# Attention's PSUM banks as eight tiles instead of four pairs, two small steps on other engines, and the order made anew

## Chip, core and metric

The kernel runs on one core of a Trainium2 chip, as one program. The metric is the device time of one execution in microseconds; the kernel before took 1075.49 us (median of three runs).

## What is computed

Three layers follow each other, all in float32. Attention works on 8 batches of 8 heads, 576 positions, 64 columns a head and 128 random features; the two dense layers on a width of 512.

```
phi(x):  proj = x @ w_phi;  proj -= max|proj| over the features;  concat(exp(proj), exp(-proj))
kv  = phi(k)^T @ v          z = sum over positions of phi(k)
x   = (phi(q) @ kv) / (phi(q) . z + 1e-6)              heads put side by side: (8, 576, 512)

xk, xr = mu_k*x + (1-mu_k)*x_prev,  mu_r*x + (1-mu_r)*x_prev     x_prev: one position earlier
x   = sigmoid(xr @ w_r) * (relu(xk @ w_k)^2 @ w_v)

gate = sigmoid(causal convolution of x over 5 positions, per column)
out  = (gate * (x @ w_val)) @ w_out
```

The weights of the dense layers and of the convolution come as 64-bit floats, read as pairs of int32.

## The kernel before

**Attention** goes over 32 pairs of heads (`NP`), two of them to a loaded block of q, k and v. For each pair TensorE projects q and k with `w_phi` (L556), VectorE takes the largest absolute value of each row (`TENSOR_REDUCE`, L562) and subtracts it (L564), ScalarE takes the exponentials. The centred q is turned by TensorE first (L621) and its exponentials are taken out of PSUM (L625). Then come `kv` (L662), `num` (L696), their copies out of PSUM (L321), a division on GpSimd and VectorE (L713, L715, L718) and the turn back (L736).

**PSUM** is held as four tiles of `[128, 2, 512]`, each two banks of 512 floats. Attention takes single banks: half `place % 2` of tile `place // 2`. The class `Banks` hands them out. The dense layers take a whole tile, one half for each half of the positions.

**The weights** are brought from 64 bits to 32 while attention runs, in 28 pieces of `[128, 512]` that `fetch` loads. `narrow` makes five steps of each: an absolute value on ScalarE (L362, `s0`), a clamp to the range of exponents on GpSimd (L365, `s1`), and three steps on VectorE (L368, L372, L376, `s2` to `s4`). GpSimd then splits the piece into a rounded part and a rest (L413, L407) for the dense products.

**The dense layers** go over 8 batches (iterations `it`), each with 624 products of 128x128 by 128x288 (L831): `st_k`, `st_r`, `st_val` of the batch before, `st_v`, and `st_out` of the batch before. The moving operands of `st_k` and `st_v` are made just in time in the tile `ops`: a rounded copy by ScalarE (L815) and the rest by VectorE (L324). `prep` loads a batch's x into the tile `xb`, whose column 0 of each of four blocks is zero (the position before the first) and is set by a memset on VectorE (L912); the load fills columns 1 to 576 of each block.

**What sets the order.** The class `Order` collects every step with its engine, a cost in microseconds, a wished time and what it reads and writes; `run` then plays the steps forward by these costs and emits, engine by engine, the one that could start first. `SEM` and `SAME` are the costs of a hand-over to another engine and to the same; `SPLIT` is added where TensorE changes to another division of its array ("rows" for the projection, "columns" for `kv` and `num`). Every engine runs its queue in the order in which it was emitted. The waits between engines are not `Order`'s: they are put in afterwards, from the tiles that each instruction touches.

```python
banks = [psum.tile([128, 2, 512], F32, tag=f"b{i}", name=f"b{i}", bufs=1) for i in range(4)]
b.places, b.tile = [place], self.pairs[place // 2][:, place % 2]
```

Of the kernel before, what the change touches and what calls it, by code (L numbers as in the profile page):

```python
# [38 lines left out]
SEM = 0.2  # L39
SAME = 0.13  # L40
# [5 lines left out]
SPLIT = 0.29  # L46
KV = 0.125
SOON, EARLY = 0.6, 0.8

# [11 lines left out]
class Banks:  # L61


    def __init__(self, pairs, most):
        self.most, self.held, self.pairs = most, [], pairs

    def when(self, tasks, new):

        live, found, out = dict.fromkeys(self.most, 0), [], set(range(2 * len(self.pairs)))
        for b in self.held:  # L70
            out.difference_update(b.places)
            ends = [tasks[u]["end"] for u in b.users]
            if None in ends:
                live[b.tag] += 1
            else:
                found += [(max(ends) + SEM, k, b) for k in b.places]
# [4 lines left out]
        if any(b.tag in LAST for b in new) and sum(live[x] for x in LAST) >= 2 * len(self.pairs):  # L81
            return None
        found = sorted([(0.0, i, None) for i in out] + found, key=lambda f: f[:2])
        if new[0].wide:
# [5 lines left out]
            return [(t, k, at[k][2]), (t, k + 1, at[k + 1][2])]  # L90
        return found[:len(new)] if len(found) >= len(new) else None

    def take(self, found, new):
        for old in {id(f[2]): f[2] for f in found if f[2] is not None}.values():
            self.held.remove(old)
        if new[0].wide:
            b = new[0]
            b.places, b.tile = [f[1] for f in found], self.pairs[found[0][1] // 2]
            self.held.append(b)
            return  # L100
        for (_, place, _), b in zip(found, new):
            b.places, b.tile = [place], self.pairs[place // 2][:, place % 2]
            self.held.append(b)
# [12 lines left out]
class Order:  # L116
# [6 lines left out]
    def add(self, eng, dur, fn, r=(), w=(), new=(), at=None, dma=0, split=False):  # L123
# [12 lines left out]
        for b in new:  # L136
            self.queue.setdefault(b.tag, []).append((b, t["id"]))
        for x in itertools.chain(r, w):
            b = x[0] if isinstance(x, tuple) else x
            if isinstance(b, Buf):  # L140
                b.users.append(t["id"])
                t["bufs"].add(b)
        t["deps"].discard(t["id"])
        self.tasks.append(t)

    def run(self):
# [3 lines left out]
        free, dma_free = {}, 0.0  # L150
        todo = {}
# [5 lines left out]
        def ready(t):  # L157
            at = 0.0
            for d in t["deps"]:
                d = tasks[d]  # L160
                if d["end"] is None:
                    return None
                at = max(at, d["end"] + (SEM if d["eng"] != t["eng"] else 0.0 if t["eng"] == "PE" else SAME))
# [9 lines left out]
            for b in t["new"]:  # L173
# [7 lines left out]
                if old >= 0:  # L181
                    for u in self.queue[b.tag][old][0].users:
                        u = tasks[u]
                        if u["end"] is None:
                            return None
                        at = max(at, u["end"] + SEM)
            return at

        left, split = len(tasks), False
        while left:  # L190
            best = None
            for eng, q in todo.items():
                f = free.get(eng, 0.0)
                got = None
                for t in q[:400]:
# [4 lines left out]
                    if eng == "PE" and split and t["split"] == split and at <= f + SOON and t["at"] <= q[0]["at"] + EARLY:  # L200
                        got = (at, t)
                        break
                    if got is None or at < got[0] - 1e-9:
                        got = (at, t)
                        if at <= f and not (eng == "PE" and split):
                            break
# [12 lines left out]
            if t["eng"] == "PE":  # L219
                if t["split"] and t["split"] != split:  # L220
                    t["dur"] += SPLIT
                split = t["split"]
            free[t["eng"]] = at + t["dur"]
# [10 lines left out]
def t_act(n):  # L234
    return n / 1200 + 0.09


def t_dve(n):
    return (n + 66) / 960


def t_dve2(n):
    return (n / 2 + 66) / 960


def t_pool(n):
    return n * 0.00225 + 0.1 * -(-n // 288)


def t_pool1(n):  # L250
    return n * 0.00115 + 0.1
# [7 lines left out]
def build(ctx, tc, qt, kt, vv, wphi, mu, wk, wr, wv, wval, cw, wout, out):  # L259
# [4 lines left out]
    psum = ctx.enter_context(tc.tile_pool(name="psum", bufs=1, space=bass.MemoryType.PSUM))  # L264
# [25 lines left out]
    banks = [psum.tile([128, 2, 512], F32, tag=f"b{i}", name=f"b{i}", bufs=1) for i in range(4)]  # L290
    G = Order(BUFS, Banks(banks, PSB))
# [58 lines left out]
    def narrow(raw, a, n, tok, new=True):  # L350
# [13 lines left out]
        def s1():  # L364
            nc.gpsimd.tensor_scalar(out=c(), in0=c(), scalar1=LEAST, scalar2=MOST, op0=ALU.max, op1=ALU.min)  # L365
# [14 lines left out]
        add("ACT", t_act(n), s0, r=[r], w=[x], new=[x] if new and isinstance(x, Buf) else [])  # L380
        add("POOL", t_pool1(n), s1, w=[x])
# [186 lines left out]
    def proj(x, j, tag):  # L568
# [8 lines left out]
        add("PE", 0.9, lambda: project(bs, x[n], [p * 512 + 128 * i for i in range(4)], 0),  # L577
# [5 lines left out]
    def tails(j):  # L583
# [8 lines left out]
        add("PE", 0.45, go, r=cols_of(qs[n], n, 2) + cols_of(ks[n], n, 2) + [("wph", 0), ("wph", 1)], w=bs, new=bs, split="rows")  # L592
# [4 lines left out]
        for half in range(2):  # L597
            add("ACT", t_act(256), lambda half=half: act(out=e[:, :, half], in_=d[:, :, 1], func=AF.Exp,
# [3 lines left out]
    def k_proj(j):  # L602
        ds = proj(ks, j, "d")
        for ab in range(2):
            d, tok = ds[ab]
            e = st[j]["ek", ab] = sb("ek", [128, 4, 2, 128])
            for half in range(2):
                add("ACT", t_act(512), lambda d=d, e=e, half=half: act(  # L608
# [96 lines left out]
    def scale(j):  # L705
# [7 lines left out]
        add("POOL", 0.15, lambda: nc.gpsimd.tensor_scalar_add(dn[:, 0:k], xn[:, 0:k, 64:65], 1e-6), r=both, w=[dn],  # L713
            new=[dn])
        add("DVE", 0.08, lambda: nc.vector.reciprocal(out=rn[:, 0:k], in_=dn[:, 0:k]), r=[dn], w=[rn], new=[rn])  # L715
# [40 lines left out]
    def moe():  # L756
# [150 lines left out]
        def prep(it):  # L907
# [293 lines left out]
```

## Time and profile before

| | |
|---|---|
| median of 3 runs (lowest, highest) | 1075.49 us (1074.37, 1080.87) |
| the profiled execution's own time | 1073.2 us |
| its span, first to last instruction | 1071.4 us |
| busy: PE, DVE, ACT, POOL | 987.8, 736.7, 638.3, 222.9 us |
| mean granted TensorE clock | 0.976 |

Attention fills the span up to about 376 us and the dense layers the rest. A share of busy time over the whole span mixes the two, so each is read by itself. PE's queue holds everything that can end the span, so its idle stretches, and what ended each of them, are what to look for; an engine that idles elsewhere matters where PE waits for it.

### The profile page before, as it was taken

The page shows a single profiled execution, that of the slowest core. Times are in us where ns is not written, and L with a number is a line of the kernel's source. Part 1 is how long each engine was busy: PE and PEld are TensorE (multiplying, and loading weights), DVE is VectorE, ACT ScalarE, POOL GpSimd, SP SyncE. Part 2 cuts the span into 40 slices and gives each one's busy share as a digit, 9 for nine tenths or more (in the row PEclk, how much of TensorE's full clock was granted, in tenths as well). Part 3 has the DMA queues.
Part 4 walks back from the last instruction along what each step waited for, and adds up shares of the span by engine and source line. Part 5 has one row for each costly group of instructions (what it writes and reads, how often), then busy time and mean ns, then how long its engine had stood idle before and what let it go on. Part 6 is the DMA issues. An engine that isn't in the chain of part 4 may idle for free.

```text
span 1071.4 us, 26797 instructions
## 1 busy us (share of the span) xinstructions
PE 987.8 (92%) x11456; PEld 953.7 (89%) x11456; DVE 736.7 (69%) x1121; ACT 638.3 (60%) x1159; POOL 222.9 (21%) x326
## 2 busy tenths in 40 slices
PE   8987897887887899998998998999999899899998
PEld 7876787777777799998998998999999899899998
DVE  6767667657866768966955874873884685588482
ACT  4765665565655787746655672683574566468351
POOL 1576669467655110000000000000000000000000
PEclk9999999999988999999999999999899999999999
DMA  7554458668774445437536725825743753582582
GB/s 200 152 172 151 134 168 237 187 189 265 228 208 144 160 155 196 158 119 269 184 108 238 244 79 201 273 87 201 247 152 119 251 191 118 206 276 80 170 283 108
DMA packets 89336, 195.81 MB, mean 183 GB/s; under 512 B 41985, under 2 KB 55681, under 8 KB 75905
## 3 DMA queue, kind: packets, MB, share of 16 engines
q1 hardware_dynamic: 84016, 184.00, 52.9%
q10 hardware_dynamic: 5200, 10.09, 2.5%
q8 instruction: 90, 1.47, 0.6%
q14 instruction: 30, 0.24, 0.1%
HBM read 161.57 MB, written 32.51 MB: 181 GB/s over the span
## 4 chain that ended last, share of the span: by engine, by line
PE 76%; DVE 9%; ACT 5%; POOL 4%; issue 4%; DMA 1%; SPq 0%; ACTq 0%; POOLq 0%; DVEq 0%
PE b L831 63%; PE b L556 4%; PE b L696 3%; PE b L662 3%; DVE ot L562 3%; DVE k L564 2%; DVE sp L564 1%; PE b L621 1%; ACT y L625 1%; POOL xf L365 1%; ACT u L608 1%; PE b L736 1%; POOL xb L407 1%; ACT x L321 1%; POOL ot L718 1%
## 5 line engine op out<-in xcount | busy, mean ns | idle before, releaser
L831 PE MATMUL b<-y,u 128*128 128x288 f32 x1536 | 206.6, 295 | 0.8 <-ACT y L815 0.4
L831 PEld LDWEIGHTS b<-y,u 128*128 128x128 f32 x1536 | 204.5, 188 | 1.3 <-ACT y L815 0.7
L831 PE MATMUL b<-ops,u 128*128 128x288 f32 x1152 | 165.0, 306 | 17.5 <-DVE ops L324 17.5
L831 PEld LDWEIGHTS b<-ops,u 128*128 128x128 f32 x1152 | 162.7, 198 | 18.9 <-DVE ops L324 18.9
L831 PE MATMUL b<-ops,wkt 128*128 128x288 f32 x1344 | 179.4, 294 | 0.0
L831 PEld LDWEIGHTS b<-ops,wkt 128*128 128x128 f32 x1344 | 178.2, 188 | 0.1
L562 DVE TENSOR_REDUCE ot<-b 128x4 f32<-128x512 f32 (+1 forms) x160 | 95.4, 626 | 56.1 <-PE b L556 36.1
L831 PE MATMUL b<-xb,u 128*128 128x288 f32 x768 | 103.0, 294 | 0.0
L831 PEld LDWEIGHTS b<-xb,u 128*128 128x128 f32 x768 | 102.2, 188 | 0.0
L809 DVE SCALAR_TENSOR_TENSOR g<-x,cwt,g 128x576 f32<-128x576 f32 x128 | 100.3, 811 | 1.0 <-ACT g L815 0.8
L556 PE MATMUL b<-wph,ops 64*128 64x128 f32 x1152 | 88.9, 296 | 11.1 <-ACT y L625 4.8
L625 ACT ACTIVATE y<-b 128x512 f32<-128x512 f32 x128 | 71.0, 598 | 44.4 <-PE b L556 13.2
L556 PEld LDWEIGHTS b<-wph,ops 64*128 64x128 f32 x1152 | 77.5, 200 | 21.8 <-ACT y L625 7.2
L696 PE MATMUL b<-g,y 128*64 128x65 f32 x2176 | 77.7, 231 | 14.8 <-ACT g L321 3.8
L696 PEld LDWEIGHTS b<-g,y 128*64 128x64 f32 x2176 | 71.8, 145 | 20.9 <-ACT g L321 4.6
L815 ACT ACTIVATE ops<-k 128x576 fp32r<-128x576 f32 x96 | 63.7, 681 | 22.6 <-PE b L831 20.8
L324 DVE TENSOR_TENSOR ops<-k,ops 128x576 fp32r<-128x576 f32 x96 | 70.1, 752 | 8.4 <-ACT ops L815 8.3
L815 ACT ACTIVATE y<-g 128x576 fp32r<-128x576 f32 x32 | 22.0, 686 | 84.8 <-DVE g L806 84.8
L815 ACT ACTIVATE k<-k 128x576 f32<-128x576 f32 x112 | 70.4, 679 | 0.1
L324 DVE TENSOR_TENSOR y<-g,y 128x576 fp32r<-128x576 f32 x32 | 24.2, 757 | 62.7 <-ACT ops L815 35.5
L806 DVE TENSOR_TENSOR g<-g,b 128x576 f32<-128x576 f32 x32 | 24.1, 754 | 57.8 <-PE b L831 57.8
L321 ACT ACTIVATE x<-b 128x260 f32<-128x260 f32 (+3 forms) x96 | 39.6, 423 | 33.9 <-PE b L696 7.2
(122 smaller groups left out, 1493.2 us busy)
## 6 DMA issues: line engine op xcount, KB each, us to landing
u<-ws SPq DMA_DIRECT2D x96, 1024.0 KB, 4.9
ws<-xb SPq DMA_DIRECT2D x24, 512.0 KB, 4.0
xs<-x SPq DMA_DIRECT2D x16, 576.0 KB, 3.9
xb<-xs SPq DMA_DIRECT2D x8, 1152.0 KB, 7.4
out<-ot ACTq DMA_DIRECT2D x32, 288.0 KB, 3.9
ops<-in_kt SPq DMA_DIRECT2D x15, 576.0 KB, 5.1
ops<-in_qt SPq DMA_DIRECT2D x15, 576.0 KB, 4.6
u<-in_vv SPq DMA_DIRECT2D x16, 512.0 KB, 4.9
```

The lines of the kernel that those rows point to most:

```text
L321: act(out=out, in_=x, func=AF.Copy)
L324: eng.tensor_tensor(out=out, in0=x, in1=hi.bitcast(F32), op=ALU.subtract)
L556: mm(out=bs[ab][:, (at + i) * 128:(at + i + 1) * 128], lhsT=x[r, c:c + 128], rhs=wph[r], start=True, stop=True)
L562: add("DVE", t_dve(128 * n), lambda: nc.vector.tensor_reduce(out=m[:, 0:n, 0], in_=b3[:, 0:n], axis=AX.X, op=ALU.max, apply_absolute_value ...
L564: add("DVE", t_dve(128 * n), lambda: tt(out=d[0](), in0=b3[:, 0:n], in1=m[:, 0:n].to_broadcast([128, n, 128]), op=ALU.subtract), r=[b, m], ...
L625: add("ACT", t_act(512), lambda half=half: act(out=e[:, ab, half, :], in_=b[:], func=AF.Exp, scale=-1.0 if half else 1.0), r=[b], w=[(e, a ...
L662: mm(out=b[y, o:o + 65], lhsT=lhs[:, y], rhs=vt[:, a:a + 65], start=(k == 0), stop=(c == 3), skip_group_check=True)
L696: mm(out=b[rows, at:at + 65], lhsT=lhs, rhs=a[:, o:o + 65], start=(k == 0), stop=(half == 1), skip_group_check=True)
L806: add("DVE", d_time(n), lambda: tt(out=out(), in0=x(), in1=y(), op=op), r=r, w=w)
L809: add("DVE", d_time(n) + 0.06, lambda: stt(out=out(), in0=x(), scalar=scalar(), in1=y(), op0=ALU.mult, op1=ALU.add), r=r, w=w)
L815: act(out=out(), in_=x(), func=func, **more)
L831: mm(out=o[:, half, 0:TB], lhsT=a, rhs=mov[b][c], start=first and k == 0, stop=last and k == n - 1, skip_group_check=True)
```

## The change

`Banks` now has eight places that are tiles of their own, `[128, 512]` each, four in a pool on the left of PSUM and four in one on the right. When the dense layers first want a wide tile of a side, that side's pool is closed and opened again as two tiles of `[128, 2, 512]`; while attention still needs banks, only one side may be wide. The clamp `s1` moves from GpSimd to VectorE. The memset of `xb` moves from VectorE to GpSimd, and the load of x is now listed as reading what the memset wrote, so that it is emitted after it. All costs of `Order` get other values, TensorE's changes of division are charged by the kind that is entered, and an engine counts as free a little before its step ends (`TAIL`). With that the order of all instructions is another.

```diff
-SEM = 0.2
-SAME = 0.13
+AFTER_PE = 0.2
+AFTER = 0.08
+SAME = 0.04
+TAIL = {"ACT": 0.1, "DVE": 0.08, "POOL": 0.05}
...
-SPLIT = 0.29
-KV = 0.125
+KV = 0.117
+ENTER = {"rows": 0.2, "columns": 0.14, "all": 0.15}
...
         if new[0].wide:
-            at = {f[1]: f for f in found}
-            two = [(max(at[k][0], at[k + 1][0]), k) for k in range(0, 2 * len(self.pairs), 2) if k in at and k + 1 in at]
+        if wide:
+            full = self.left and any(self.paired)
+            at = {f[1]: f for f in found if self.paired[f[1] // 4] or not (full or stuck[f[1] // 4])}
+            two = [(max(at[k][0], at[k + 1][0]), k) for k in range(0, 8, 2) if k in at and k + 1 in at]
...
         for (_, place, _), b in zip(found, new):
-            b.places, b.tile = [place], self.pairs[place // 2][:, place % 2]
+            b.places, b.tile = [place], self.single(place)
...
-    banks = [psum.tile([128, 2, 512], F32, tag=f"b{i}", name=f"b{i}", bufs=1) for i in range(4)]
-    G = Order(BUFS, Banks(banks, PSB))
+    sides = [ExitStack(), ExitStack()]
+    single, double = {}, {}
+    for i, side in enumerate(("left", "right")):
+        p = sides[i].enter_context(tc.tile_pool(name=f"s{i}", bufs=1, space=bass.MemoryType.PSUM, side=side))
+        for k in range(4 * i, 4 * i + 4):
+            single[k] = p.tile([128, 512], F32, tag=f"b{k}", name=f"b{k}", bufs=1)
+
+    def pair(k):
+        i = k // 2
+        if k not in double:
+            sides[i].close()
+            p = ctx.enter_context(tc.tile_pool(name=f"p{i}", bufs=1, space=bass.MemoryType.PSUM,
+                                               side=("left", "right")[i], reuse_waits="tile"))
+            for a in range(2 * i, 2 * i + 2):
+                double[a] = p.tile([128, 2, 512], F32, tag=f"c{a}", name=f"c{a}", bufs=1)
+        return double[k]
+
+    G = Order(BUFS, Banks(lambda k: single[k], pair, PSB))
...
         def s1():
-            nc.gpsimd.tensor_scalar(out=c(), in0=c(), scalar1=LEAST, scalar2=MOST, op0=ALU.max, op1=ALU.min)
+            nc.vector.tensor_scalar(out=c(), in0=c(), scalar1=LEAST, scalar2=MOST, op0=ALU.max, op1=ALU.min)
...
-        add("POOL", t_pool1(n), s1, w=[x])
+        add("DVE", t_dve2(n), s1, w=[x])
...
-            add("DVE", 0.07, lambda: nc.vector.memset(x()[:, :, 0:1], 0.0), r=[("page", "xb")], w=["x0"])
+            add("POOL", 0.15, lambda: nc.gpsimd.memset(x()[:, :, 0:1], 0.0), r=[("page", "xb")], w=["x0"])
             load(lambda: x()[:, :, 1:577], lambda: xs[it].rearrange("c d s -> d c s"), 1179648,
-                 r=[("xs", it, c) for c in range(2)], w=x.tok)
+                 r=[("xs", it, c) for c in range(2)] + ["x0"], w=x.tok)
```

Lines of the changed kernel are numbered anew: the projection is L589, the reduction L595, the subtraction L597, the turn L654, `kv` L695, `num` L729, the turn back L769, the products L864, ScalarE's and VectorE's helpers L848, L839, L842 and L357, the memset of `xb` L945, the clamp L398.

**The turn of q, head pair 8, TensorE and VectorE.** `sp` holds the centred q, `ot` the row maxima, `k2` the centred k; `b0_80` to `b3_83` are the four paired PSUM tiles. TensorE before:

```order
L662 MATMUL b2_82<-u1_73,k2_71 64x65 [waits DMAHW4_49]
L662 MATMUL b2_82<-u1_73,k2_71 64x65 x15
L662 MATMUL b2_82<-u1_73,u0_72 64x65 x16
L621 MATMUL b0_80<-ident_86,sp_70 128x128 [waits DVE_49]
L621 MATMUL b0_80<-ident_86,sp_70 128x128 x3
L634 MATMUL b1_81<-ident_86,k2_71 128x128 [waits DVE_49,Activation_49]
```

The same stretch on VectorE before, whose first row reads one half of `b0_80` and whose third waits for TensorE:

```order
L562 TENSOR_REDUCE ot_78<-b0_80 128x4
L562 TENSOR_REDUCE ot_78<-b1_81 128x4
L564 TENSOR_TENSOR k2_71<-b0_80,ot_78 128x512 [waits DVE_49,PE_49]
L564 TENSOR_TENSOR k2_71<-b1_81,ot_78 128x512 [waits DVE_49,PE_49]
L368 TENSOR_SCALAR xf_67<-xf_67 128x512 [waits Pool_49] x2
```

And TensorE at the turn of the same head pair now, where `b0_80` to `b7_90` are eight single banks:

```order
L695 MATMUL b5_88<-u1_70,k2_68 64x65 x15
L695 MATMUL b5_88<-u1_70,u0_69 64x65 x16
L729 MATMUL b2_82<-g_74,y_72 64x65 [waits DVE_49]
L729 MATMUL b2_82<-g_74,y_72 64x65 x15
L729 MATMUL b2_82<-g_74,x2_73 64x65 x8
L654 MATMUL b3_83<-ident_93,sp_67 128x128 [waits DVE_49]
L654 MATMUL b3_83<-ident_93,sp_67 128x128 x3
L654 MATMUL b1_81<-ident_93,sp_67 128x128 [waits DVE_49]
```

The turn stood right behind `kv` in a half of a tile whose other half VectorE was reading; now a `num` stands between, and the turn goes to tiles of its own.

**The memset of `xb`, between `st_val` and `st_v` of an iteration.** `g` is the gate, `y` the operand of `st_out`, `ops` those of `st_v`. VectorE before:

```order
L806 TENSOR_TENSOR g_5036<-g_5036,b1_81 128x576 [waits PE_49]
L324 TENSOR_TENSOR y_4997<-g_5036,y_4997 128x576 [waits Activation_49]
L806 TENSOR_TENSOR g_5036<-g_5036,b2_82 128x576 [waits PE_49]
L912 MEMSET xb_6055 128x4 [waits DMAHW3_49]
L324 TENSOR_TENSOR y_4997<-g_5036,y_4997 128x576 [waits Activation_49]
L324 TENSOR_TENSOR ops_4799<-k2_4934,ops_4799 128x576 [waits Activation_49] x3
L806 TENSOR_TENSOR sp_4868<-sp_4868,b3_83 128x576 [waits PE_49]
```

VectorE at the same place now:

```order
L357 TENSOR_TENSOR y_4987<-g_5033,y_4987 128x576 [waits Activation_49]
L839 TENSOR_TENSOR g_5033<-g_5033,c1_5051 128x576 [waits PE_49]
L357 TENSOR_TENSOR y_4987<-g_5033,y_4987 128x576 [waits Activation_49]
L357 TENSOR_TENSOR ops_4812<-k2_4926,ops_4812 128x576 [waits Activation_49] x3
L839 TENSOR_TENSOR sp_4875<-sp_4875,c0_5050 128x576 [waits PE_49]
```

The memset, which waited for a DMA in front of the operands, is gone from VectorE's queue. It now stands on GpSimd, whose last work for attention is the two rows ahead of it:

```order
L751 TENSOR_TENSOR ot_75<-x2_73,g_74 128x4x64 [waits Pool_49]
L755 TENSOR_TENSOR ot_75<-x2_73,g_74 128x128 [waits PE_49]
L945 MEMSET xb_5171 128x4 [waits DMAHW7_49,DVE_49]
L945 MEMSET xb_6074 128x4 [waits DVE_49,PE_49,DMAHW5_49,Activation_49,Pool_49]
L945 MEMSET xb_6888 128x4 [waits DVE_49,DMAHW3_49,PE_49,Pool_49]
```

And SyncE's load of x waits for GpSimd now, at the same place between the loads of `u`:

```order
L375 DMA u1_4660<-ws_106 128x2048 [waits DMAHW5_49,PE_49]
L375 DMA u2_4928<-ws_106 128x2048 [waits DMAHW7_49,PE_49]
L375 DMA xb_6074<-xs2_100 128x4x576 [waits Pool_49]
L375 DMA u0_4927<-ws_106 128x2048 [waits DMAHW0_49,PE_49]
L375 DMA u1_4660<-ws_106 128x2048 [waits DMAHW1_49,PE_49]
```

What moved is the memset alone; the loads keep their places.

**The clamp, VectorE, early in attention.** `xf` holds a piece of the weights. Before, the shift L368 waited for GpSimd's clamp (the last row of the second fence). Now:

```order
L597 TENSOR_TENSOR sp_67<-b4_87,ot_75 128x512 [waits DVE_49]
L748 RECIPROCAL g_74<-ot_75 128x8 [waits Pool_49]
L398 TENSOR_SCALAR xf_64<-xf_64 128x512 [waits Activation_49]
L401 TENSOR_SCALAR xf_64<-xf_64 128x512 [waits DVE_49]
L595 TENSOR_REDUCE ot_75<-b6_89 128x4 [waits PE_49]
L595 TENSOR_REDUCE ot_75<-b7_90 128x4 [waits PE_49]
```

Clamp and shift follow each other on VectorE, between a reciprocal and the next reductions, and the wait for GpSimd has become one for ScalarE's absolute value.

## Rows read from the trace of the kernel before

**Rows 1.** Windows: busy time (instructions) of each engine by stage, clock, DMA

```profile
0.00:376.00 376.00, 314.38 (x6460) 282.44 (x6461) 257.34 (x466) 224.81 (x487) 219.57 (x322) 0.96 0.62 186
376.00:488.00 112.00, 112.00 (x846) 111.90 (x846) 81.46 (x111) 78.10 (x129) 3.29 (x4) 1.00 0.47 164
488.00:928.00 440.00, 422.50 (x3123) 421.11 (x3122) 304.71 (x419) 261.64 (x426) 0.00 (x0) 0.98 0.54 185
```

**Rows 2.** Waits from 14 to 381 us: us in total, times, longest

```profile
DVE ot L562 <- ACT y L625: 13.2, 6, 5.7
PE b L621 <- DVE ot L562: 6.6, 4, 2.1
DVE xf L368 <- POOL xf L365: 6.5, 4, 2.5
PE b L556 <- DVE ot L562: 3.8, 2, 3.4
PE b L696 <- ACT g L321: 3.8, 4, 1.4
PE b L696 <- DVE ot L562: 2.9, 4, 1.1
PE b L736 <- POOL x L718: 2.2, 4, 1.4
PE b L736 <- DVE ot L562: 1.8, 2, 1.3
PE b L634 <- DVE ot L562: 1.5, 2, 1.2
```

**Rows 3.** Timeline about 104 us: start, length, work [idle before it <- releaser]

```profile
102.60 1.29 DVE L564 TENSOR_TENSOR sp<-b,ot 128x512 f32<-128x512 f32 x2 [2.46 <-PE b L662]
...
103.93 1.23 DVE L562 TENSOR_REDUCE ot<-b 128x4 f32<-128x512 f32 x2
...
104.61 0.66 PE L621 MATMUL b<-ident,sp 128*128 128x128 f32 x4 [2.06 <-DVE ot L562]
...
105.30 1.29 DVE L564 TENSOR_TENSOR k<-b,ot 128x512 f32<-128x512 f32 x2
```

**Rows 4.** Waits of PE from 381 us to the end

```profile
PE b L831 <- DVE ops L324: 17.5, 6, 3.3
```

**Rows 5.** Timeline from 480 to 494 us

```profile
482.10 0.43 SPq L342 DMA_DIRECT2D xb<-xs  x1
...
486.59 0.69 ACT L815 ACTIVATE ops<-k 128x576 fp32r<-128x576 f32 x1 [0.38 <-PE b L831]
...
489.53 0.75 DVE L324 TENSOR_TENSOR y<-g,y 128x576 fp32r<-128x576 f32 x1 [7.04 <-ACT ops L815]
489.55 0.06 DVE L912 MEMSET xb<- 128x4 f32 x1
490.19 2.09 DVE L324 TENSOR_TENSOR ops<-k,ops 128x576 fp32r<-128x576 f32 x3
...
491.00 3.21 PE L831 MATMUL b<-ops,u 128*128 128x288 f32 x15 [2.78 <-DVE ops L324]
```

**Rows 6.** DMA issues: KB each, median us from issue to landing

```profile
xb<-xs SPq DMA_DIRECT2D x8, 1152.0 KB, 7.4
```

**Rows 7.** Windows from one stall's end to the next one's start, columns as in 1

```profile
491.00:575.50 84.50, 84.50 (x624) 84.30 (x624) 59.13 (x80) 51.53 (x84) 0.00 (x0) 0.98 0.53 181
578.80:661.80 83.00, 82.98 (x624) 82.78 (x624) 59.01 (x80) 51.54 (x84) 0.00 (x0) 1.00 0.53 182
...
752.10:837.80 85.70, 85.68 (x624) 85.49 (x624) 59.25 (x80) 51.53 (x84) 0.00 (x0) 0.96 0.52 178
```

**Rows 8.** GpSimd's clamp L365 and subtraction L407, by line: busy, mean ns

```profile
L365 POOL TENSOR_SCALAR xf<-xf 128x512 f32<-128x512 f32 x19 | 36.9, 1946 | 26.9 <-ACT xf L362 26.8
L407 POOL TENSOR_TENSOR xb<-xf,xb 128x256 fp32r<-128x256 f32 (+1 forms) x36 | 28.1, 794 | 0.8
```

**Rows 9.** VectorE's two-step shift L368: ns min/median/max

```profile
L368 DVE TENSOR_SCALAR xf<-xf x19: 416/422/812, 27.4 to 338.0; 128x512 int32<-128x512 int32 x19
```

**Rows 10.** Chain of waits: TensorE in runs of `num`, start, length

```profile
22.01 1.14 PE b L696 x32
...
26.91 2.08 PE b L696 x64
```

More of the change, by code (lines that the diff above doesn't have):

```diff
@@ L61, with __init__ @@
 class Banks:
-    def __init__(self, pairs, most):
-        self.most, self.held, self.pairs = most, [], pairs
+    def __init__(self, single, pair, most):
+        self.most, self.held, self.single, self.pair, self.paired = most, [], single, pair, [False, False]
+        self.left = 0
     def when(self, tasks, new):
-        live, found, out = dict.fromkeys(self.most, 0), [], set(range(2 * len(self.pairs)))
+        wide = new[0].wide
+        live, found, out = dict.fromkeys(self.most, 0), [], set(range(8))
+        stuck = [False, False]
         for b in self.held:
@@ L74, in when @@
                 live[b.tag] += 1
+                stuck[b.places[0] // 4] = True
             else:
-                found += [(max(ends) + SEM, k, b) for k in b.places]
+                found += [(max(tasks[u]["end"] + lag(tasks[u]["eng"], "PE") for u in b.users), k, b) for k in b.places]
         for b in new:
@@ L90, in when @@
             return [(t, k, at[k][2]), (t, k + 1, at[k + 1][2])]
+        if any(b.tag in LAST for b in new) and sum(live[x] for x in LAST) >= 8 - 4 * sum(self.paired):
+            return None
+        found = [f for f in found if not self.paired[f[1] // 4]]
         return found[:len(new)] if len(found) >= len(new) else None
@@ L97, in take @@
             b = new[0]
-            b.places, b.tile = [f[1] for f in found], self.pairs[found[0][1] // 2]
+            b.places = [f[1] for f in found]
+            self.paired[b.places[0] // 4] = True
+            b.tile = self.pair(b.places[0] // 2)
             self.held.append(b)
             return
+        self.left -= len(new)
         for (_, place, _), b in zip(found, new):
-            b.places, b.tile = [place], self.pairs[place // 2][:, place % 2]
+            b.places, b.tile = [place], self.single(place)
             self.held.append(b)
@@ L121, in __init__, with add @@
         self.last_write, self.reads, self.now = {}, {}, 0.0
-    def add(self, eng, dur, fn, r=(), w=(), new=(), at=None, dma=0, split=False):
+    def add(self, eng, dur, fn, r=(), w=(), new=(), at=None, dma=0, split="all"):
         t = {"eng": eng, "dur": dur, "fn": fn, "deps": set(), "at": self.now if at is None else at,
@@ L150, in run @@
         free, dma_free = {}, 0.0
+        self.banks.left = sum(not b.wide for tag in self.banks.most for b, _ in self.queue.get(tag, ()))
         todo = {}
@@ L185, in ready @@
                             return None
-                        at = max(at, u["end"] + SEM)
+                        at = max(at, u["end"] + lag(u["eng"], t["eng"]))
             return at
-        left, split = len(tasks), False
+        left, shape = len(tasks), None
         while left:
@@ L204, in run @@
                         got = (at, t)
-                        if at <= f and not (eng == "PE" and split):
+                        if at <= f and not (eng == "PE" and shape != "all"):
                             break
@@ L219, in run @@
             if t["eng"] == "PE":
[L220 to L223, printed above, removed]
+                if t["split"] != shape:
+                    t["dur"] += ENTER[t["split"]]
+                shape = t["split"]
+            free[t["eng"]] = at + t["dur"] - TAIL.get(t["eng"], 0.0)
             t["end"] = at + t["dur"]
@@ L590, in go @@
                 project(bs, x[n], [1024], i)
-        add("PE", 0.45, go, r=cols_of(qs[n], n, 2) + cols_of(ks[n], n, 2) + [("wph", 0), ("wph", 1)], w=bs, new=bs, split="rows")
+        add("PE", 0.42, go, r=cols_of(qs[n], n, 2) + cols_of(ks[n], n, 2) + [("wph", 0), ("wph", 1)], w=bs, new=bs, split="rows")
         for ab in range(2):
```

36 lines of the change are left out of this document (18 added, 18 removed).

## The prediction

> **What bounds the kernel.** I first split the span by stage [rows 1]. In the first 376 us, attention, TensorE is busy for 314.4 us and idle for 61.6; VectorE is busy for 257.3 (68%), GpSimd for 219.6. The dense layers come next: no idle time at all to 488 us, then 17.5 us of it in 440. So TensorE is what ends last in both stages, and its idle time is the most that a change of order can win: some 62 us in attention and 17.5 in the dense layers, plus what the clock loses (below).
>
> Then I asked what ended the idle time. In attention the list of waits [rows 2] has pairs that make no sense by the data. TensorE waits for the reduction L562 in five places, together 6.6 + 3.8 + 2.9 + 1.8 + 1.5 = 16.6 us. Yet the reduction is never the last reader of a bank: L564 reads the same bank after it, so no freed bank and no result that TensorE uses comes from L562. Just as odd, the reduction itself waits 13.2 us for ScalarE's exponentials L625, though all it reads is TensorE's product. The order shows why. At the turn of head pair 8, TensorE writes `b0_80`, VectorE reduces `b0_80` right then, and the subtraction that follows waits for TensorE: two banks, but halves of one tile. The timeline there [rows 3] shows the turn starting at 104.61, after 2.06 us of idling, in the midst of the two reductions (103.93 to 105.16), and the next subtraction at 105.30, just when the turn is over (104.61 + 0.66). The planner `Order` treats the halves as free of each other; the waits, put in by tile, do not. These are false waits.
>
> In the dense layers there is one wait only: the operands' rest L324, 17.5 us in six places [rows 4]. The timeline of one [rows 5] shows VectorE idle for 7.04 us just ahead. ScalarE had rounded the operands in time (one of them at 486.59). What held VectorE is the memset: it writes column 0 of `xb` while the load of `xb`, issued at 482.10, fills the rest, and it waits until that load has landed. 482.10 plus 7.4 [rows 6] is 489.5, and the memset stands at 489.55. The engine named in brackets had long been done.
>
> **The dense layers, part by part.** The memset goes to GpSimd, idle there, ahead of the load. VectorE loses 8 x 0.06 us and, which matters, the wait. Six stalls go: -17.5 us. Each also costs clock: between two stalls TensorE makes 624 products, in 83.0 us where the granted clock is 1.00, in 84.5 and 85.7 where it is 0.98 and 0.96, that is, where it fell to the lower level, 1.2 GHz, after the idle stretch [rows 7]. The five such stretches (first and last shown; the others 84.5 and 84.2) exceed 83.0 by 6.9 us together, and I add 1.4, their mean, after the sixth stall: -8.3. Sum -25.8, with bounds of -20 (another operand is late by a microsecond each time) and -27. What is late next? Without the stall TensorE reaches ScalarE's first use of x some 2.8 us earlier relative to the load, which now waits for a hand-over to GpSimd and back, a few tenths. In the trace that use comes over 4 us after the landing, so about 1 us of slack is left; I cost the moved load at nothing, and at 1 us an iteration, 8 in all, if that cover is gone. Behind the load on SyncE's queue stand only loads of `u`, in the old order.
>
> **Attention's eight tiles.** The new order has no wait for another half. Of TensorE's 61.6 us, 16.6 are certainly false. At most the rest of the list could be (35 pairs, 57.6 us, of which [rows 2] shows the largest), less what must be true: 3.8 for `num` behind the copy of `kv`, 2.2 for the turn back behind GpSimd, and 6.9 more of such kinds; that leaves about 45. Going through TensorE's waits of over 60 ns one by one with the order, I count some 42 us in which the only thing missing was an access to the other half, so I take a value near the upper end. Not all of it comes back: VectorE would be busy for some 270 of 340 us, 80%, and a true wait takes part of the place. I take five sixths, -35, the short list of true waits speaking for so much, and keep -10 and -45 as bounds. The tighter order changes TensorE's division more often: 167 runs of one kind up to the last turn back where there were 153. A run of 32 products of `num` took 1.14 us and one of 64 took 2.08 [rows 10], so entering one costs 2 x 1.14 - 2.08 = 0.2 and 14 more cost +2.8.
>
> **The clamp.** GpSimd loses 28 x 1.95 = 54 us of 219.6 [rows 8]. VectorE gets 28 clamps; the shift L368, the same kind of instruction on the same shape, takes 0.42 at the median and 0.81 at most [rows 9], which makes 28 x 0.42 = 12 to 23 us. In return VectorE no longer stands for GpSimd's clamp: 6.5 us for `xf` [rows 2], and as much again for the two other places. I cost the exchange at 0 on the path, between -6 and +10: TensorE sees it only where a reduction is queued behind.
>
> That shift takes 0.42 us most often and 0.81 at times [rows 9], so something stretches it. The Trainium skill (SBUF — State Buffer, "Who interferes with whom") says that such an instruction of VectorE and one of GpSimd lock each other out: the second to issue is blocked until the first ends. By that rule a clamp on VectorE may each time stand for a whole GpSimd instruction beside it, which is 0.79 us in the row of L407 [rows 8]; as an estimate from rule and row, 28 x (0.42 + 0.79) = 34 us in place of 12, and the time would be some 20 us longer if all of it were on the path. The median of 0.42 in the row agrees with it only for the few slow ones, so the sum stays by the row.
>
> **Sum.** 1073.2 - 25.8 - 35 + 2.8 + 0 = 1015.2 against the profiled execution. That one lies 2.3 us below the median of the three, so I expect a median of about 1017.
>
> **The rivals.** (1) VectorE becomes the bound of attention. It is at 68% now; with the clamps and a stage shorter by a tenth it passes 80%, and its queue holds the reductions that everything waits for. Then attention wins only the lower bound, 10, and the time is 1073 - 26 - 10 + 3 + 2 = 1042. For it: VectorE's share. Against it: 13.2 us of its idling is itself false and goes [rows 2]. (2) The eight tiles bring more: all 42 to 45 come back, and hand-overs costed closer to the trace fill some true waits as well, as does the clock, 0.96 in attention [rows 1]. Some 50 us: 1000. (3) The change does not do what it says in the dense layers: x arrives later because the load now stands behind GpSimd, ScalarE stands at the first use of x, and the stall only changes its name. Then the 26 stay and the time is about 1043. Against it: 7.4 us of landing with 4 us of slack, and a queue of GpSimd that is empty. (4) The clamps are all stretched as the slowest shift was: 28 x 0.81 = 23 us more for VectorE, all of it on the path and no wait for GpSimd given back, 1017 + 23 = 1040; the trace has most shifts at 0.42, with GpSimd far busier. The lock in the Trainium skill's page on SBUF, named above, would be its mechanism. (5) Slower than before: the clamp carries its wait into VectorE's queue. On GpSimd it stood 26.8 us for ScalarE's absolute value [rows 8], which waits for a piece's load. If VectorE, whose queue holds the reductions, stands there as long, and for 14 us more under the clamps themselves, 41 us land on the path; with nothing from the eight tiles that is 1073 - 26 + 41 + 2 = 1090. It decides from where the clamp is emitted before its piece has landed more than a dozen times.
>
> **Chances and range.** Forecast 0.58 (1005 to 1030), rival 2 0.17, rival 1 0.12, rival 3 with smaller failures 0.06, rival 4 0.03, rival 5 0.04. A measurement of this kernel tells about 1% from no change. Faster than 1064.7 are all but the last and half of the smaller failures: 0.93; within 1% 0.03; slower 0.04. The range of 996 to 1042 takes in rival 4, and most of rivals 1 and 2.
>
> **What would show it.** In the dense layers: no wait of the products for operands of several microseconds, VectorE's rests of operands right after ScalarE's roundings, 83.0 us an iteration with a clock of 1.00, the memset on GpSimd before the load. In attention: no wait of TensorE or ScalarE for the reduction; TensorE's idle time some 25 us instead of 61.6; the end of attention at about 344 us. VectorE busy for some 270 us before that. The forecast fails if attention's idle time keeps its size under other names (VectorE's subtractions or the copies of ScalarE), or if the first use of x becomes the wait of each iteration.

## The result and the profile after

The changed kernel takes 980.29 us (median of four runs, 977.95 to 984.26), the kernel before 1075.53 beside it: ratio 0.911, 95% interval 0.907 to 0.915. The forecast was 1017 with a range from 996, so the gain was under-estimated by 37 us. The profiled execution took 979.43 us, its span is 977.6.

Both profiles are cut at the end of the last turn back on TensorE, 380.6 us before and 312.9 now. The windows of the kernel before, attention and then the rest, cut there (columns as in [rows 1]):

```profile
0.00:380.60 380.60, 318.98 (x6495) 286.95 (x6496) 261.73 (x472) 228.98 (x494) 222.86 (x326) 0.96 0.62 186
380.60:1071.40 690.80, 668.80 (x4963) 666.71 (x4961) 474.93 (x650) 409.32 (x665) 0.00 (x0) 0.99 0.53 181
```

The same two of the changed kernel:

```profile
0.00:312.90 312.90, 294.59 (x6483) 269.39 (x6484) 267.71 (x495) 222.19 (x490) 173.80 (x298) 1.00 0.73 226
312.90:977.60 664.70, 660.27 (x4975) 659.59 (x4973) 479.64 (x648) 407.37 (x669) 0.73 (x7) 1.00 0.55 188
```

The dense layers lose 26.1 us, forecast 25.8. Attention loses 67.7, forecast 32. The miss is all there, and the row splits it: TensorE's idle time falls from 61.6 to 18.3 us (-43.3), and its busy time from 319.0 to 294.6 (-24.4), for which the forecast had only +2.8 the other way. The granted clock went from 0.96 to 1.00.

TensorE's waits in attention now, largest first, answer to [rows 2]:

```profile
PE b L769 <- POOL ot L751: 3.6, 4, 1.2
PE b L729 <- ACT g L354: 2.0, 2, 1.7
PE b L695 <- issue: 2.0, 2, 1.3
PE b L729 <- issue: 1.9, 3, 0.8
PE b L654 <- DVE sp L597: 1.6, 2, 1.0
```

No line names the reduction (L595 now). What is left are true waits: the turn back for GpSimd's scaled `x`, `num` for ScalarE's copy. VectorE's wait for the exponentials, 13.2 us in [rows 2], is down to 0.5:

```profile
DVE ot L595 <- ACT y L658: 0.5, 1, 0.5
```

VectorE is busy for 267.7 of 312.9 us, 86%, and still isn't what ends last.

The timeline of a dense iteration (PE, SyncE, GpSimd, ScalarE) answers to [rows 5]:

```profile
415.73 0.11 POOL L945 MEMSET xb<- 128x4 f32 x1 [91.66 <-PE c L864]
415.93 0.43 SPq L375 DMA_DIRECT2D xb<-xs  x1
...
418.56 7.63 PE L864 MATMUL c<-ops,u 128*128 128x288 f32 x56
...
422.02 0.69 ACT L848 ACTIVATE ops<-k 128x576 fp32r<-128x576 f32 x1 [0.91 <-PE c L864]
422.74 0.76 DVE L357 TENSOR_TENSOR ops<-k,ops 128x576 fp32r<-128x576 f32 x1
...
424.15 1.43 ACT L848 ACTIVATE xf<-xb,mut 128x576 f32<-128x576 f32 x2
```

The memset stands 0.2 us ahead of the load. VectorE's rest follows ScalarE's rounding at once (422.02 + 0.69 = 422.71, then 422.74), where [rows 5] has it standing for 7.04 us. Counted with its 7.4 us [rows 6], the load ends at about 423.3; ScalarE uses `xb` at 424.15, so the slack is 0.8 us.

### The profile page after: what moved, and what is told of

Same layout as the page of the kernel before. It is cut to its first block, busy times and chain, and to the rows that moved or that the text cites. A ratio compares the mean times of both kernels' runs of the same rounds, so it can differ in the third digit from the quotient of the medians.

```text
span 977.6 us, 26826 instructions
## 1 busy us (share of the span) xinstructions
PE 954.9 (98%) x11456; PEld 929.0 (95%) x11456; DVE 747.3 (76%) x1142; ACT 629.6 (64%) x1159; POOL 174.5 (18%) x305
## 4 chain that ended last, share of the span: by engine, by line
PE 82%; DVE 6%; POOL 4%; DMA 4%; ACT 2%; issue 2%; SPq 1%; ACTq 0%; POOLq 0%; DVEq 0%
PE c L864 67%; PE b L695 5%; PE b L589 3%; PE b L729 3%; DVE ot L595 2%; PE b L654 1%; DMA xb<-in_wout 1%; PE b L769 1%; DVE k L597 1%; POOL wkt L440 1%; POOL xf L440 1%; SPq L375 1%; DVE sp L597 1%; DMA xb<-in_wv 1%; ACT y L658 1%
## 5 line engine op out<-in xcount | busy, mean ns | idle before, releaser
L864 PE MATMUL c<-y,u 128*128 128x288 f32 x1536 | 206.6, 295 | 0.8 <-ACT y L848 0.4
L864 PEld LDWEIGHTS c<-y,u 128*128 128x128 f32 x1536 | 204.5, 188 | 1.3 <-ACT y L848 0.7
L864 PE MATMUL c<-ops,wkt 128*128 128x288 f32 x1344 | 179.3, 294 | 0.0
L864 PEld LDWEIGHTS c<-ops,wkt 128*128 128x128 f32 x1344 | 178.2, 188 | 0.0
L864 PE MATMUL c<-ops,u 128*128 128x288 f32 x1152 | 154.9, 295 | 0.0
L864 PEld LDWEIGHTS c<-ops,u 128*128 128x128 f32 x1152 | 154.0, 188 | 0.0
L595 DVE TENSOR_REDUCE ot<-b 128x4 f32<-128x512 f32 (+1 forms) x160 | 94.2, 625 | 19.6 <-PE b L589 18.9
L864 PE MATMUL c<-xb,u 128*128 128x288 f32 x768 | 103.0, 294 | 0.0
L864 PEld LDWEIGHTS c<-xb,u 128*128 128x128 f32 x768 | 102.2, 188 | 0.0
L842 DVE SCALAR_TENSOR_TENSOR g<-x,cwt,g 128x576 f32<-128x576 f32 x128 | 100.1, 813 | 1.6 <-ACT g L848 0.8
L945 POOL MEMSET xb<- 128x4 f32 x8 | 0.8, 105 | 519.8 <-PE c L864 504.8
L357 DVE TENSOR_TENSOR ops<-k,ops 128x576 fp32r<-128x576 f32 x96 | 72.5, 755 | 19.4 <-ACT ops L848 18.7
L839 DVE TENSOR_TENSOR g<-g,c 128x576 f32<-128x576 f32 x32 | 24.1, 754 | 76.2 <-PE c L864 76.2
L589 PE MATMUL b<-wph,ops 64*128 64x128 f32 x1152 | 78.7, 281 | 1.3 <-ACT x L354 0.6
L848 ACT ACTIVATE ops<-k 128x576 fp32r<-128x576 f32 x96 | 64.8, 682 | 21.7 <-PE c L864 21.0
L589 PEld LDWEIGHTS b<-wph,ops 64*128 64x128 f32 x1152 | 69.5, 188 | 8.2 <-issue 4.1
L729 PEld LDWEIGHTS b<-g,y 128*64 128x64 f32 x2176 | 67.0, 137 | 9.9 <-issue 4.9
L729 PE MATMUL b<-g,y 128*64 128x65 f32 x2176 | 72.1, 223 | 4.5 <-ACT g L354 2.0
L848 ACT ACTIVATE y<-g 128x576 fp32r<-128x576 f32 x32 | 21.9, 686 | 84.5 <-DVE g L839 84.5
L848 ACT ACTIVATE k<-k 128x576 f32<-128x576 f32 x112 | 70.6, 680 | 1.9 <-DVE k L839 1.9
L848 ACT ACTIVATE x<-c 128x576 f32<-128x576 f32 x32 | 20.9, 653 | 55.6 <-PE c L864 54.9
```

The costliest lines, as they stand in the source:

```text
L357: eng.tensor_tensor(out=out, in0=x, in1=hi.bitcast(F32), op=ALU.subtract)
L589: mm(out=bs[ab][:, (at + i) * 128:(at + i + 1) * 128], lhsT=x[r, c:c + 128], rhs=wph[r], start=True, stop=True)
L595: add("DVE", t_dve(128 * n), lambda: nc.vector.tensor_reduce(out=m[:, 0:n, 0], in_=b3[:, 0:n], axis=AX.X, op=ALU.max, apply_absolute_value ...
L729: mm(out=b[rows, at:at + 65], lhsT=lhs, rhs=a[:, o:o + 65], start=(k == 0), stop=(half == 1), skip_group_check=True)
L839: add("DVE", d_time(n), lambda: tt(out=out(), in0=x(), in1=y(), op=op), r=r, w=w)
L842: add("DVE", d_time(n) + 0.06, lambda: stt(out=out(), in0=x(), scalar=scalar(), in1=y(), op0=ALU.mult, op1=ALU.add), r=r, w=w)
```

## The experiments

The theory after the result: (a) the eight tiles take away the false waits, and with the idle time goes the loss of clock; (b) with the false waits gone, GpSimd's queue is late ahead of the turn back, so the clamp's move pays, though it pays nothing alone; (c) the memset is worth its 26 us on its own; (d) the new costs matter little. The rivals: the new order did it, or the clamp by itself. The ratios are to the kernel before as measured again beside each group of runs; its median there was 1071 to 1074 us, and 1076 beside the result, so a few microseconds between runs of different groups say little. Wherever an edit changes a step's engine or cost, `Order` also makes a new order, so those runs show the edit and its order together.

**The memset alone.** The kernel before with

```diff
-            add("DVE", 0.07, lambda: nc.vector.memset(x()[:, :, 0:1], 0.0), r=[("page", "xb")], w=["x0"])
+            add("POOL", 0.15, lambda: nc.gpsimd.memset(x()[:, :, 0:1], 0.0), r=[("page", "xb")], w=["x0"])
...
-                 r=[("xs", it, c) for c in range(2)], w=x.tok)
+                 r=[("xs", it, c) for c in range(2)] + ["x0"], w=x.tok)
```

> The kernel before with only the memset moved to GpSimd ahead of the load. By the theory of the dense layers (six stalls of 17.5 us and 8.3 us of lower clock): 1075.5 - 26 = 1049, no wait of the products for operands, 83.0 us an iteration. By the rival (the load comes later and the first use of x becomes the wait): 1070 or more.

Measured 1046.3 us, ratio 0.976 (0.971 to 0.980). Its windows:

```profile
0.00:380.60 380.60, 317.74 (x6496) 285.60 (x6497) 258.23 (x467) 226.97 (x491) 222.74 (x327) 0.96 0.61 186
380.60:1043.80 663.20, 658.69 (x4963) 658.00 (x4961) 481.10 (x647) 410.59 (x668) 0.73 (x7) 1.00 0.55 188
```

Attention ends where it did; the dense layers lose 27.6 us and run at clock 1.00. Of these, 17.5 are idle time (22.0 to 4.5) and 10.1 busy time. Part (c) holds.

**The tiles alone.** The kernel before with the changed kernel's `Banks` and eight tiles, the old costs, and so the old order of attention, instruction by instruction:

```diff
-    banks = [psum.tile([128, 2, 512], F32, tag=f"b{i}", name=f"b{i}", bufs=1) for i in range(4)]
...
+            single[k] = p.tile([128, 512], F32, tag=f"b{k}", name=f"b{k}", bufs=1)
```

> The kernel before with only the PSUM banks of attention as eight tiles; attention's order is that of before, instruction by instruction, and so are costs, clamp and memset. If the false waits and the clock that they cost are what attention lost, most of the 68 us that it became shorter by come here: 1015 to 1030, and the clock stays at 1.00 in attention. If it is the order made anew by better costs, under 25 us: 1050 or more.

Measured 1032.86 us, ratio 0.961 (0.955 to 0.966): 41 us from tiles alone, with attention's order kept (only about its end do some steps of VectorE and ScalarE change places). Attention's window:

```profile
0.00:341.50 341.50, 302.51 (x6496) 276.75 (x6497) 260.51 (x472) 225.12 (x494) 223.93 (x326) 0.98 0.68 207
```

The gain is less than expected and the clock 0.98, not 1.00; the waits say why (of TensorE, largest first):

```profile
PE c L856 <- DVE ops L349: 17.7, 6, 3.4
PE b L761 <- POOL ot L743: 10.9, 6, 3.2
PE b L761 <- POOL x L743: 10.0, 6, 4.3
PE b L687 <- issue: 2.7, 3, 1.3
```

The first line is the memset's, untouched. The next two, 20.9 us, are the turn back standing for GpSimd. Before, it was 3.7: the 2.2 of [rows 2] and

```profile
PE b L736 <- POOL ot L718: 1.5, 3, 0.8
```

The longest of them in the timeline, GpSimd and then TensorE:

```profile
126.97 1.92 POOL L390 TENSOR_SCALAR tmp<-tmp 128x512 f32<-128x512 f32 x1
128.87 1.91 POOL L390 TENSOR_SCALAR xb<-xb 128x512 f32<-128x512 f32 x1
130.75 1.36 POOL L743 TENSOR_TENSOR x<-x,g 128x256 f32<-128x256 f32 x2
```

```profile
132.16 1.12 PE L761 MATMUL b<-ident,x 128*128 128x128 f32 x4 [4.25 <-POOL x L743]
```

Two clamps stand ahead of the scaling that the turn back reads, and TensorE idles for 4.25 us. GpSimd is busy for only 224 of 341 us: it is late by what stands in its queue, not for want of time.

**The new order on paired tiles.** The changed kernel in its own order, each bank again a half:

```diff
...
+    banks = [psum.tile([128, 2, 512], F32, tag=f"b{i}", name=f"b{i}", bufs=1) for i in range(4)]
+    single = {k: banks[k // 2][:, k % 2] for k in range(8)}
...
```

> The changed kernel with the four paired tiles back under attention's banks, the order of every engine being that of the changed kernel. By the theory of the false waits: 40 to 70 us slower than 980, 1020 to 1050, with waits of TensorE for the reduction and a clock under 1.00 in attention. By the rival of the order: under 1000.

Measured 1057.58 us, ratio to before 0.985 (0.981 to 0.990), 77 us over the changed kernel where 40 to 70 had been expected. Attention's window and TensorE's largest waits:

```profile
0.00:389.30 389.30, 318.26 (x6484) 285.04 (x6485) 274.16 (x495) 228.21 (x490) 173.72 (x298) 0.96 0.59 182
```

```profile
PE b L579 <- ACT y L648: 8.1, 7, 3.0
PE b L719 <- DVE ot L585: 6.8, 6, 3.7
PE b L579 <- DVE k L587: 5.1, 5, 2.0
PE b L657 <- DVE ot L585: 4.7, 3, 1.8
```

The reduction (L585 here) is back as a releaser. Attention takes 389.3 us, more than the 380.6 of the old order, so order and clamp together, without the tiles, are worth nothing there.

**The memset put back** in the changed kernel (the first diff reversed).

> The changed kernel with the memset back on VectorE behind the load. By the theory of the dense layers: stalls of some 2.8 us and a lower clock after them, 980 + 26 = 1006. If the new order of the dense layers hides the wait: 980 to 985.

Measured 1012.32 us, ratio to before 0.943 (0.939 to 0.947), 32 us over the changed kernel, 6 more than expected. Its largest wait is the old one of [rows 4], and the next one is a wait that the changed kernel doesn't have:

```profile
PE c L864 <- DVE ops L357: 16.7, 6, 2.9
PE c L864 <- ACT k L848: 3.2, 1, 3.2
```

The rival, that the new order hides the wait, falls.

**Tiles and clamp.** The run with the tiles alone and

```diff
-            nc.gpsimd.tensor_scalar(out=c(), in0=c(), scalar1=LEAST, scalar2=MOST, op0=ALU.max, op1=ALU.min)
+            nc.vector.tensor_scalar(out=c(), in0=c(), scalar1=LEAST, scalar2=MOST, op0=ALU.max, op1=ALU.min)
...
-        add("POOL", t_pool1(n), s1, w=[x])
+        add("DVE", t_dve2(n), s1, w=[x])
```

> The kernel before with two of the edits: eight one-bank tiles and the clamp on VectorE (planner's costs and the memset as before, so the dense layers keep their 690.9 us). Theory: with the tiles alone TensorE's remaining idle time in attention, 39.0 us, came for 20.9 us from GpSimd's queue ahead of the turn back, in which a clamp takes 1.95 us; without clamps there that part goes, attention takes about 320 us and the run about 1012 us. Rival: GpSimd was late for its own copies and the clamps mattered little, or VectorE becomes late instead: 1025 to 1040 us, with the idle time of attention still over 30 us.

Measured 1013.23 us, ratio 0.945 (0.940 to 0.951), 20 us under the run with the tiles alone (16 by the ratios). TensorE's waits for GpSimd at the turn back fall from 20.9 to 5.5 us, attention takes 321.6. One idle stretch of 6.2 us remains there, and it is the memset's; VectorE's timeline, between SyncE's load and TensorE:

```profile
289.54 0.36 SPq L367 DMA_DIRECT2D xb<-xs  x1
```

```profile
286.45 0.19 DVE L740 RECIPROCAL g<-ot 128x8 f32<-128x8 f32 x1
297.47 0.69 DVE L587 TENSOR_REDUCE ot<-b 128x4 f32<-128x512 f32 x1 [10.83 <-DMA xb<-xs]
297.48 0.06 DVE L937 MEMSET xb<- 128x4 f32 x1
```

```profile
299.41 3.78 PE L581 MATMUL b<-wph,ops 64*128 64x128 f32 x30 [6.20 <-DVE k L589]
```

The first load of a dense batch is issued while attention still runs. The memset holds VectorE until it lands, with attention's reductions queued behind.

**The clamp alone**, on the kernel before (the same edit).

> The kernel before with the clamp alone on VectorE: four two-bank tiles, planner's costs and memset as before. The prediction put this at nothing, between 6 us less and 10 us more. Theory: while two halves of a tile wait for each other, GpSimd's queue is not what is late (in the kernel before its waits take 2.2 us of TensorE's time), so the time stays within 6 us of before, about 1074 us. Rival: the clamps pay by themselves, since the division's chain gets 1.5 us shorter each time: 1050 to 1060 us.

Measured 1079.14 us, ratio 1.004 (1.000 to 1.007): nothing to a slight loss, within the prediction's bounds. The rival falls.

**The clamp back on GpSimd** in the changed kernel, at its true price:

```diff
-            nc.vector.tensor_scalar(out=c(), in0=c(), scalar1=LEAST, scalar2=MOST, op0=ALU.max, op1=ALU.min)
+            nc.gpsimd.tensor_scalar(out=c(), in0=c(), scalar1=LEAST, scalar2=MOST, op0=ALU.max, op1=ALU.min)
...
-        add("DVE", t_dve2(n), s1, w=[x])
+        add("POOL", 0.2 + 0.00342 * n, s1, w=[x])
```

> The changed kernel with the clamp on GpSimd again, and told to the planner with the time that it takes there (0.2 us and 3.42 ns a column). Theory: GpSimd is the bound of attention again; with the tiles alone it cost 20.9 us of idle time, so about 1000 us, and TensorE's waits at the turn back name GpSimd. Rival: the planner, now knowing the true time, hides it: 980 to 985 us.

Measured 988.93 us, ratio 0.921 (0.915 to 0.926), 9 us over the changed kernel. That is nearer to the rival: a planner that knows the 1.95 us puts clamps where they hold nobody up, for the most part (9.3 us of waits at the turn back for GpSimd's `ot` and `x`, where the changed kernel has 4.1).

**The true price in the old order.** To see whether that also explains the 20 us, the run with the tiles alone, with only this changed:

```diff
-        add("POOL", t_pool1(n), s1, w=[x])
+        add("POOL", 0.2 + 0.00342 * n, s1, w=[x])
```

> The run with the eight tiles alone, but with the clamp's true price on GpSimd told to the planner (0.2 us and 3.42 ns a column, 1.95 us for 512 columns, where the old formula has 0.69 us). Theory A: what cost 20 us there was the wrong price, an order with clamps too close ahead of the turn back; with the true price about 1015 us, near the 1013.2 us with the clamp on VectorE. Theory B: GpSimd is short of time whatever the order, so it stays at 1025 to 1033 us.

Measured 1022.34 us, ratio 0.956 (0.952 to 0.960): between the two theories. Attention takes 332.5 us in its profile, beside 341.5 with the tiles alone and 321.6 with the clamp moved, so the price would be about half of the gain there. By the ratios it is a third (0.961, 0.956, 0.945), and its interval overlaps with that of the tiles alone: how the 20 us divide is not settled.

**The old costs.** The changed kernel with `SEM`, `SAME`, `SPLIT` and the old cost functions:

> The changed kernel with the planner's costs of before: eight tiles, clamp on VectorE and memset on GpSimd, in the order that the old costs give. Theory: the order made by the new costs is worth little once the tiles are there, since those costs alone take no wait away: 980 to 990 us. Rival: the order carries a third or more of the gain in attention: 1000 us or more. It should also come out 27 us below the run with the tiles and the clamp alone, the price of the memset.

Measured 985.28 us, ratio 0.918 (0.913 to 0.922), beside 0.911 (0.907 to 0.915) of the changed kernel. The windows:

```profile
0.00:315.40 315.40, 294.81 (x6490) 269.89 (x6491) 267.45 (x496) 222.70 (x490) 171.56 (x298) 1.00 0.73 225
315.40:979.40 664.00, 659.50 (x4969) 658.81 (x4967) 481.56 (x647) 411.75 (x669) 0.74 (x7) 1.00 0.55 188
```

Attention is 2.5 us longer than in the changed kernel, the dense layers are the same. By the medians the new costs bring 5 us, by the profiled spans 1.8; the intervals overlap, so no gain of theirs is shown. The memset is worth 28 us on top of tiles and clamp, 6.2 of them in attention (321.6 to 315.4), the stretch shown above.

**The new costs alone**, on the kernel before:

> The kernel before with the planner's new costs alone, and so a new order; two-bank tiles, clamp and memset as before. Theory: the costs say nothing about the two halves of a tile waiting for each other, so a new order with two-bank tiles meets as many false waits as the old one or more: 1065 to 1090 us, dense layers at 691 us. Rival: the new costs are what makes attention faster, at least 15 us: 1058 us or less.

Measured 1080.65 us, ratio 1.010 (1.007 to 1.013). The windows:

```profile
0.00:378.00 378.00, 315.12 (x6484) 281.67 (x6485) 258.73 (x467) 227.93 (x490) 222.24 (x326) 0.97 0.61 187
378.00:1076.80 698.80, 673.60 (x4974) 671.27 (x4973) 476.82 (x655) 408.18 (x669) 0.00 (x0) 0.98 0.52 179
```

The order by itself makes the kernel a little slower, and not in attention, which is 2.6 us shorter than before: the dense layers are 8 us longer. With the memset on VectorE, an order made with the new costs takes longer there (696.5 us in the run with the memset put back) than the old one (690.8).

**A version that might beat both.** The changed kernel with

```diff
-DMA_END = 1.0
-DMA_RATE = 350e3
+DMA_END = 1.3
+DMA_RATE = 250e3
```

> A version that might beat the changed kernel: its planner is told DMA times nearer to the trace (end after 1.3 us for 1.0, 250 GB/s for 350 GB/s, worked out from a 512 KB weight piece that lands in 4.4 to 5.1 us and the load of x that lands in 7.4 us); nothing else is changed. Theory: ScalarE stands behind weight pieces that land later than planned, and the 18.3 us that TensorE still idles in attention come partly from that: 970 to 976 us. Rival: what is left is start, end and the turn's own chain, so 980 us within 5 us.

Measured 1022.35 us, ratio 0.954 (0.951 to 0.958), 42 us worse than the changed kernel. Its windows and TensorE's largest waits:

```profile
0.00:312.40 312.40, 294.50 (x6464) 268.60 (x6464) 262.90 (x484) 214.58 (x477) 174.38 (x297) 0.99 0.72 222
312.40:1020.40 708.00, 673.79 (x4992) 669.73 (x4992) 490.59 (x659) 415.67 (x682) 0.84 (x8) 0.98 0.51 179
```

```profile
PE c L864 <- ACT ops L848: 12.3, 1, 12.3
PE c L864 <- ACT ot L848: 11.6, 6, 1.9
```

Attention ends 0.5 us earlier, with 19 products fewer ahead of the cut (6464 for 6483), so telling the planner of later weight pieces wins nothing of its last 18 us of idle time. The order after it, which the same two numbers set, gets new waits for ScalarE: idle time up from 4.4 to 34.2 us, clock down to 0.98. The 12.3 us are where attention gives way to the dense layers; SyncE and ScalarE there:

```profile
314.97 0.36 SPq L375 DMA_DIRECT2D xb<-xs  x1
```

```profile
320.61 2.77 ACT L848 ACTIVATE xf<-xb,mut 128x576 f32<-128x576 f32 x4 [7.92 <-DMA xb<-xs]
```

The first dense batch's load of `xb` is issued at 314.97, behind the end of attention; in the changed kernel its memset stands at 287.1, 26 us ahead of that end. Both theories missed this. Why the shorter waits came, 0.9 and 1.9 us in each iteration, stays open. No version beat the changed kernel.

## Why the prediction fell short

**The dense layers** were right as told: 17.5 of stalls and 8.3 of clock made -25.8, measured -26.1 in the changed kernel and -27.6 alone. The memset alone shows 17.5 of idle time and 10.1 of busy time, so the clock's term was 2 short. That -26.1 comes out so near is in part luck: 12 dense products, some 1.6 us, now come after the cut and were ahead of it before (4963 and 4975 in the windows, 0.13 us each). The slack at the load, put at about 1 us, is 0.8. The rival of a renamed stall falls.

**Attention** is where it failed, in the term "I take five sixths, -35". Three parts of TensorE's time were mis-sized; they make up the 67.7: 43.3 of idle time, 15.2 of clock, 9.2 of busy time besides. The table has, run by run, attention's length, TensorE's idle and busy time in it, and an estimate of what the clock cost (one less the granted clock, times the length; the clock has two digits, so it is good to about 2 us):

| run | attention | idle | busy | clock's loss | busy less clock's loss |
|---|---|---|---|---|---|
| before | 380.6 | 61.6 | 319.0 | 15.2 | 303.8 |
| clamp alone | 385.2 | 66.4 | 318.8 | 15.4 | 303.4 |
| new costs alone | 378.0 | 62.9 | 315.1 | 11.3 | 303.8 |
| new order, paired tiles | 389.3 | 71.0 | 318.3 | 15.6 | 302.7 |
| tiles alone | 341.5 | 39.0 | 302.5 | 6.8 | 295.7 |
| tiles, true price | 332.5 | 29.3 | 303.2 | 10.0 | 293.2 |
| tiles and clamp | 321.6 | 24.4 | 297.2 | 3.2 | 294.0 |
| clamp back | 322.4 | 22.3 | 300.1 | 6.4 | 293.7 |
| old costs | 315.4 | 20.6 | 294.8 | 0.0 | 294.8 |
| changed kernel | 312.9 | 18.3 | 294.6 | 0.0 | 294.6 |

- *The clock.* The sum counted it in the dense layers and left it out in attention, though [rows 1] had 0.96 there; it stood only in the second rival. 0.04 x 380.6 = 15 us went with the idle stretches.
- *Busy time besides the clock.* The four runs with two-bank tiles have 303 to 304 us of it, the six with one-bank tiles 293 to 296. Two pairs of runs have the same order and differ in the tiles alone: before and the tiles alone (303.8 and 295.7), paired tiles in the new order and the changed kernel (302.7 and 294.6). So 8 us go with the tiles, give or take the 2 us of the clock; what is left of the 9.2 is no more than the 12 dense products above. Why the tiles do this is not shown. What the traces offer: TensorE's work in attention is broken by an idle stretch 84 times before and 42 times with the tiles alone, 85 times on paired tiles in the new order and 29 in the changed kernel, so fewer products stand at the start of a stretch, where their full length shows. An estimate with the 0.2 us that the prediction took from [rows 10] for such a start gives 8 us for the first pair and 11 for the second. The mean projection product went from 296 ns (with the low clock in it) to 281.
- *The idle time.* -43.3 in place of -35. With the tiles alone it fell by 22.6 only, since GpSimd's queue was next: waits at the turn back for its `ot` and `x` rose by 17.2 (3.7 to 20.9). Together that is 40 us, near the 42 counted as false; that all of them were is not shown one by one. With the clamp moved too, nothing took a sixth of their place. (The list of 35 pairs adds up to 56.7 us, not 57.6; its upper end would be 44.)

Put one on the other, the edits shorten attention by 39.1 us (tiles, 380.6 to 341.5), 19.9 (clamp, to 321.6), 6.2 (memset, to 315.4) and 2.5 (new costs, to 312.9). The prediction had the memset's part in the dense layers alone. In another order of adding the shares would differ: taken first, the clamp is worth nothing.

**The clamp**, costed at 0 with bounds of -6 and +10, is 0 to +7 alone and about -20 behind the tiles; put back into the changed kernel at its true price, it costs 9. The step that failed is that its price was read in the kernel before: which wait is late next was asked of VectorE (the first rival), not of GpSimd. VectorE's own side was right: 28 clamps take 14.1 us (12 to 23 told), mean 0.50, and VectorE waits for ScalarE's absolute value ahead of them for 10.1 us, not the 26.8 of the last rival. The rule of the Trainium skill (SBUF — State Buffer, "Who interferes with whom") would have shown as clamps stretched by GpSimd's work:

```profile
L398 DVE TENSOR_SCALAR xf<-xf x19: 376/427/947, 23.4 to 275.7; 128x512 f32<-128x512 f32 x19
```

The median is 0.43 and the maximum 0.95 us, so a few may have waited and most did not; it is not the price here.

**The division's changes**, +2.8, can't be found: attention's busy time less the clock's loss is the same in the order with the old costs (294.8, 155 runs of one kind) and the new (294.6, 167). But the new order has 7 products fewer ahead of its cut, some 0.9 us, so a cost of a microsecond or two may hide there.

**The rivals.** VectorE as the bound falls: it is 86% busy, yet TensorE's waits for it in attention come to 3.7 us in all. The second, that the tiles bring more and the clock with them, had the mechanism right in the main, without GpSimd's queue, but at 1000 us still too small a gain. The range missed for a reason that is plain now: its lower end took in the second rival's 50 us, when 62 of idle time and 15 of clock stood in one row.

## What to carry to other kernels

When a stall on the bounding engine goes, count its clock in every stage by the same row (one less the granted clock, times the stretch: in [rows 7] that gives 1.7 and 3.4 us where 84.5 and 85.7 exceed 83.0 by 1.5 and 2.7). When many waits go at once, look for the next late queue on every engine, and price an edit with the others made: the clamp's move was worth nothing before the tiles, and 20 us or, in an order that knew its price, 9 behind them. A planner may treat two halves as free of each other only if they are two tiles; otherwise the waits undo its order (the changed kernel's order takes 389.3 us of attention on pairs and 312.9 on tiles of one bank).

## What was not expected of the hardware

- Short idle stretches go with a lower clock: in the last run TensorE stands twice in a dense iteration, for 0.9 and 1.9 us. Of three iterations, cut from one stall of 1.9 us to the next, two have a granted clock of 0.98 (85.7 and 85.8 us) and one of 1.00 (84.2 us):

```profile
476.40:562.10 85.70, 84.79 (x624) 84.38 (x624) 59.41 (x80) 49.87 (x82) 0.10 (x1) 0.98 0.54 187
564.10:648.30 84.20, 83.30 (x624) 82.84 (x624) 59.30 (x81) 49.58 (x82) 0.10 (x1) 1.00 0.55 190
650.20:736.00 85.80, 84.85 (x624) 84.38 (x624) 59.48 (x81) 49.98 (x82) 0.10 (x1) 0.98 0.54 187
```

- A `tensor_scalar` with two operations on 128x512 floats takes 1.95 us on GpSimd [rows 8] and 0.43 at the median on VectorE, on the same tiles.
